# The second batch's key products moved into the first transform, in place of warm-up products; weight roundings moved beside the second layer; activation tables loaded in idle stretches

## The chip, the cores and the metric

One core of one Trainium2 chip (trn2), float32 throughout. The time is the device time of one execution, in microseconds (us), as the median of several executions. Ratios are the mean time of one kernel's fast runs over the mean time of the other's fast runs of the same rounds, with a 95% interval, so they are not quite the ratio of the medians that stand beside them. A trace belongs to one execution out of several.

## The reference

Eight batches of 576 tokens with 512 columns pass through linear attention, a two-dimensional Fourier mix, a normalisation and a two-layer perceptron:

```python
q_s = softmax(q over its 64 columns);  k_s = softmax(k over the 576 tokens)
x   = q_s @ (k_s^T @ v)                        # per batch and head; 8 heads of 64
u   = x + real(fft(fft(x, over tokens), over columns))
un  = (u - mean) / sqrt(var + 1e-6)
out = u + relu(un @ w1) @ w2                   # w1 512 x 2048, w2 2048 x 512
```

The weights arrive as 64-bit floats and are turned into float32 ("rounded") on the chip, block by block, by ScalarE, VectorE and GpSimd together.

## The kernel before

Rows of several batches form groups. Group 0 runs the two layers plainly; later groups use pre-combined weights and fewer products. While TensorE runs group g, the attention and transform of the next batch are mixed in between its products. "Batch 1" is the second batch and "batch 2" the third, counting from 0. A builder with its own estimates of durations decides the final order of each engine's instructions, so build order and run order differ. Line numbers in profiles are those of the kernel named; here is what the argument touches (cuts marked).

```python
def k_exp(self, it):                                    # one key tile: 2 heads, 128 x 576
    V.reduce_max(m[:], k, axis=AX.X, negate=True)                        # "km"
    nc.scalar.activation(k, k, ACT.Exp, bias=m[:, 0:1], accum_out=rec[:, 0:1])
    ...
def k_turn(self, it):                                   # four transposes, a copy, one more
    nc.scalar.copy(ks[:, 0:4, :], pt[:])                                 # "ks <- tr"
    ...
def k_times_v(self, it):                                # five products -> "kvr"
    ...
def block(k):                                           # one block of the transform
    ... three products into pz ...
    nc.scalar.copy(paired(z), ...)                                       # "Z <- acc"
    nc.scalar.mul(paired(zt[:, at:at + Q]), ...)                         # "ZT <- acc"
    nc.scalar.copy(paired(zt[:, at + Q:at + W]), ...)                    # "ZT <- acc"
    ...
def scales(s):                                          # in norm(g)
    nc.scalar.activation(std[:, s], mv[:, s, 1], ACT.Sqrt, bias=self.eps[:, 0:1])
    ...
def normal(i):                 # g == 0: VectorE; later groups: ScalarE, "eo <- x,mv,std"
    ...
def turn(i):                   # transposes of the normalised tile, then
    nc.scalar.copy(unT[:, u:u + 3:2, :, cols], ...)                      # "unT <- tr"
...
blk.first(fetch)               # batch 0's loads, then the weights
free = blk.hold()
one, two = front(0)            # attention; transform and mixing
for step in one + two + norm(0):
    step()
```

TensorE was kept busy in the first transform by products whose results nobody uses (`self.warm(...)`), meant to keep its granted clock up (the mean was 0.97 from 0 to 61 us). Batch 1's keys were loaded and multiplied during group 0's second layer.

## Time and profile before

| | us |
|---|---|
| median, lowest, highest of the first three runs | 1142.15, 1141.45, 1142.95 |
| span of the profiled run | 1140.2 |
| first matmul of layer one (group 0) | 61.02 |
| layer one of group 0 | 56.19 |
| layer two of group 0, with batch 1 mixed in | 83.41 |
| start of group 1 | 200.62 |
| end of the last sum on VectorE | 1133.04 |

The table is read off the TensorE timeline: the first product on `unT` with 512 columns opens layer one, the first `bc<-big` with 512 columns opens layer two, the first product on `unT` with 256 columns opens group 1. A line of a timeline has the start, the duration, the engine, line and operation, the output and inputs, the shapes and the count; in brackets stands how long the engine was idle before it and which instruction ended that. The profile lines that carry the argument stand in the prediction below.

### The profile page before, as it was taken

The numbers are of one execution on the slowest core, as the hardware profiler recorded it, in microseconds if no ns is written. First come the engines' busy times: TensorE is split into PE (matmuls) and PEld (weight loads), VectorE is DVE, ScalarE is ACT, GpSimd is POOL, SyncE is SP. The second block draws the span as 40 slices with busy tenths as digits, with TensorE's granted clock in tenths as the row PEclk, the third lists the DMA queues.
The fourth block names the chain that finished last, engine by engine and source line by source line (L and its number), as shares of the span: only waits on it lengthen the run. The fifth ranks groups of instructions, "written<-read, shape, count | busy, mean of one in ns | idle before, by whom it ended". The sixth has DMA issues, their size and how long they took to land.

```text
span 1140.2 us, 14639 instructions
## 1 busy us (share of the span) xinstructions
PE 1098.6 (96%) x5472; PEld 919.1 (81%) x5472; DVE 543.4 (48%) x1110; ACT 397.7 (35%) x956; POOL 332.5 (29%) x302
## 2 busy tenths in 40 slices
PE   5899999989999999999999999999999999999997
PEld 4644556878888988888889888888889888888886
DVE  6785756488324833384435643683344352203201
ACT  6495423274124513371226322641233142201200
POOL 2075541245012600324024402260034213302320
PEclk9999999999999999999999999999999999999999
DMA  9377784463346534554356436543453344444451
GB/s 310 120 258 243 258 279 148 149 213 140 122 150 206 202 111 143 183 195 154 124 176 213 148 113 190 195 172 107 143 191 148 114 163 148 185 139 154 150 185 55
DMA packets 92549, 193.79 MB, mean 170 GB/s; under 512 B 23088, under 2 KB 59696, under 8 KB 85312
## 3 DMA queue, kind: packets, MB, share of 16 engines
q1 hardware_dynamic: 90680, 191.82, 49.5%
q10 hardware_dynamic: 1800, 1.05, 0.3%
q8 instruction: 43, 0.70, 0.2%
q14 instruction: 26, 0.21, 0.1%
HBM read 168.72 MB, written 28.31 MB: 173 GB/s over the span
## 4 chain that ended last, share of the span: by engine, by line
PE 79%; DVE 11%; ACT 4%; DMA 2%; issue 2%; POOL 1%; SPq 0%; ACTq 0%; POOLq 0%; DVEq 0%
PE bb L850 14%; PE bb L886 13%; PE bc L886 10%; PE bc L850 9%; PE ba L850 9%; PE ba L886 8%; PE acc L484 3%; PE acc L564 2%; PE bc L789 2%; PE acc L655 2%; PE acc L658 2%; PE acc L678 1%; PE tr L750 1%; PE tr L532 1%; PE tr L467 1%
## 5 line engine op out<-in xcount | busy, mean ns | idle before, releaser
L850 PE MATMUL bb<-unT,big 128*128 128x256 f32 x768 | 187.9, 381 | 0.3 <-DVE u L822 0.3
L886 PE MATMUL bb<-big 128*128 128x256 f32 x768 | 172.8, 379 | 0.0
L850 PEld LDWEIGHTS bb<-unT,big 128*128 128x128 f32 x768 | 142.8, 190 | 23.8 <-DVE u L818 3.4
L886 PEld LDWEIGHTS bb<-big 128*128 128x128 f32 x768 | 145.1, 190 | 20.1
L341 POOL TENSOR_TENSOR big<-big 128x512 f32<-128x512 f32 (+1 forms) x38 | 45.1, 1187 | 309.5 <-ACT big L862 305.6
L850 PE MATMUL bc<-unT,big 128*128 128x256 f32 x512 | 125.3, 379 | 0.0
L850 PE MATMUL ba<-unT,big 128*128 128x256 f32 x512 | 124.3, 379 | 0.0
L862 ACT ACTIVATE big<-big 128x512 f32<-128x512 f32 x96 | 60.2, 628 | 171.3 <-DVE big L861 171.0
L886 PE MATMUL bc<-big 128*128 128x256 f32 x512 | 116.5, 379 | 0.5 <-DVE x L903 0.5
L886 PE MATMUL ba<-big 128*128 128x256 f32 x512 | 114.1, 379 | 0.0
L886 PEld LDWEIGHTS bc<-big 128*128 128x128 f32 x512 | 95.9, 190 | 14.1 <-DVE x L903 0.9
L886 PEld LDWEIGHTS ba<-big 128*128 128x128 f32 x512 | 95.9, 190 | 12.3
L850 PEld LDWEIGHTS bc<-unT,big 128*128 128x128 f32 x512 | 95.5, 190 | 12.5
L850 PEld LDWEIGHTS ba<-unT,big 128*128 128x128 f32 x512 | 95.0, 190 | 11.7
L822 DVE TENSOR_TENSOR u<-bb,s 128x512 f32<-128x512 f32 x40 | 27.6, 689 | 134.8 <-PE bb L886 79.1
L521 ACT ACTIVATE q<-q,qm 128x64 f32<-128x64 f32 x240 | 61.5, 337 | 10.2 <-DVE qm L519 9.4
L349 POOL TENSOR_TENSOR unT<-unT 128x512 f32<-128x512 f32 x8 | 14.2, 1773 | 172.9 <-DVE unT L348 172.9
L818 DVE TENSOR_TENSOR u<-bb,s 128x512 f32<-128x512 f32 x40 | 27.6, 690 | 76.8 <-PE bb L850 38.1
L898 POOL TENSOR_TENSOR x<-x,u 128x512 f32<-128x512 f32 x14 | 17.7, 1267 | 148.2 <-DVE u L822 118.0
L861 DVE TENSOR_TENSOR big<-bc,u 128x512 f32<-128x512 f32 x64 | 44.1, 688 | 26.1 <-PE bc L850 25.3
L814 ACT COPY s<-ba 128x512 f32<-128x512 f32 x40 | 23.4, 584 | 89.4 <-PE ba L886 45.5
L754 ACT COPY unT<-tr 128x512 f32<-128x512 f32 x36 | 20.6, 585 | 86.5 <-PE tr L750 86.0
(221 smaller groups left out, 1656.7 us busy)
## 6 DMA issues: line engine op xcount, KB each, us to landing
big<-w1s SPq DMA_DIRECT2D x64, 896.0 KB
big<-w2s SPq DMA_DIRECT2D x56, 1024.0 KB
big<-in_w_dram SPq DMA_DIRECT2D x21, 512.0 KB
k<-in_kT_dram SPq DMA_DIRECT2D x26, 288.0 KB
q<-in_q_dram SPq DMA_DIRECT2D x27, 256.0 KB
v<-in_v_dram SPq DMA_DIRECT2D x26, 256.0 KB
words<-in_w_dram SPq DMA_DIRECT2D x11, 512.0 KB
w2s<-big SPq DMA_DIRECT2D x8, 512.0 KB
```

The source lines that it names most:

```text
L341: e1.tensor_tensor(out=to(4), in0=at(2), in1=at(3), op=ALU.add)
L484: nc.tensor.matmul(pk, lhsT=ks[:, c, :], rhs=v[:, c, :], start=(c == 0), stop=(c == NC - 1))
L521: nc.scalar.activation(heads[:, h, :], heads[:, h, :], ACT.Exp, bias=m[:, h:h + 1])
L564: nc.tensor.matmul(px[:, r * P:(r + 1) * P], lhsT=qT[:, r, :], rhs=self.kvr[b % 2][:, r, :], start=True, stop=True)
L655: nc.tensor.matmul(full[:, at:at + size], lhsT=t[:, own], rhs=self.ft[:, f + at:f + at + size], start=at == 0, stop=False, skip_group_chec ...
L814: nc.scalar.copy(temp("s1"), box["ba"][:])
L818: V.tensor_tensor(out=temp("u2"), in0=box["bb"][:], in1=box["s1"][:], op=ALU.add)
L822: V.tensor_tensor(out=temp("u3"), in0=box["bb"][:], in1=box["s1"][:], op=ALU.add)
L850: nc.tensor.matmul(bank()[:, i, :], lhsT=w[:, WA_AT[m], k * P:(k + 1) * P], rhs=unT[:, B_AT[m], k, :], start=first and i == 0 and k == 0, ...
L861: V.tensor_tensor(out=hp(i), in0=bank[:], in1=u[:], op=ALU.add)
L862: nc.scalar.activation(hp(i), hp(i), ACT.Relu)
L886: nc.tensor.matmul(bank()[:, i, :], lhsT=h[p][:, A_AT[m], i * P:(i + 1) * P], rhs=w[:, p, :], start=first and i == 0 and p == 0, stop=p == ...
```

## The change

The intent: TensorE is idle for a third of the first 61 us and full afterwards, so work taken from the full stretch into the early one should shorten the whole. The core of the diff (cut):

```diff
+        for r in range(NR):                      # in first(): batch 1's k and v ahead of the weights
+            load(self.second_at[0][:, r * S:(r + 1) * S], self.kT[1, cols, :])
+            ...
+    def second_keys(self):                       # maxima, exponentials, square-root table load, products
+        ...
-                if b == 0:
-                    self.warm(x[:, 0:HD], 3)     # warm-up products of the mixing
-            self.wait_for(eo[1][:, NN:], [self.raws[i] for i in range(4)])
+            self.wait_for(eo[1][:, NN:], [self.raws[0]])          # 1 block rounded here, not 4
+                if i == 0:
+                    self.gate(un[:], words[0:1, 1:4, 0:2])        # blocks 1-3 wait for the first un
+            if g > 0:                            # in norm: Exp table right behind the square root
+                nc.scalar.activation(t[:], std[:, 0:1], ACT.Exp, scale=0.0)
-        held = {12: [("k", S, 2)] * 2, 14: [("q", D, 3)] * 3}
+        held = {12: [("q", D, 3)] * 3, 15: [("k", S, 2)] * 2 + [("v", NC * P, 2)] * 2}
+            order = (1, 0) if last and m == 3 else (0, 1)         # tail: the halves change places
-        return folds + [lambda k=k: block(k) for k in (2, 3, 0, 1, 4)]
+        return folds + [lambda: None] * (b > 1) + [lambda k=k: block(k) for k in (2, 3, 0, 1, 4)]
-    for step in one + two + norm(0):
+    for step in one + keys + two + products + norm(0):
-            n = 2 * NF - 8
+            n = 2 * NF - 14                      # fewer roundings beside layer one, more beside layer two
```

## The prediction

> **What bounds the kernel now.** I read the page first, then stretches of the span, then the TensorE timeline with its waits, then ScalarE, VectorE and the DMA issues around each wait, and the end of the chain of waits. From the page and from the stretches (columns: us, then busy us and count of PE, PEld, DVE, ACT, POOL, then granted clock, DMA share, GB/s):

> ```profile
> PE 1098.6 (96%) x5472; PEld 919.1 (81%) x5472; DVE 543.4 (48%) x1110; ACT 397.7 (35%) x956; POOL 332.5 (29%) x302
> ...
> 0.00:61.00 61.00, 40.52 (x234) 33.76 (x235) 44.12 (x127) 36.11 (x102) 10.28 (x30) 0.97 0.65 204
> 61.00:117.20 56.20, 55.23 (x128) 24.34 (x129) 36.03 (x65) 40.02 (x71) 35.84 (x30) 1.00 0.78 253
> 117.20:200.60 83.40, 79.22 (x329) 47.29 (x328) 55.49 (x130) 31.70 (x88) 31.94 (x38) 1.00 0.68 232
> 200.60:1128.00 927.40, 919.59 (x4768) 810.75 (x4766) 406.88 (x789) 289.91 (x696) 254.49 (x205) 1.00 0.46 159
> 1128.00:1140.20 12.20, 4.07 (x18) 2.96 (x16) 0.85 (x2) 0.00 (x0) 0.00 (x0) 0.80 0.16 43
> ```

> TensorE sets the time from 61 us on: the first layer of group 0 runs to 117.2, its second layer, with all of batch 1's attention and transform mixed in, to 200.6, the other groups to 1132.6. After 200.6 only 7.8 us are idle before 1128. Before 61 us TensorE is idle for 20.5 us, and some of the rest is junk. So two things pay: work taken out of the full stretch into the first 61 us, and waits removed. The TensorE timeline shows both:

> ```profile
> 46.52 0.61 PE L678 MATMUL acc<-cd,Z 127*128 127x127 f32 x4
> 49.48 7.13 PE L206 MATMUL tr<-x,ident 128*128 128x256 f32 x24 [2.35 <-DVE x L696]
> ...
> 61.02 3.67 PE L780 MATMUL ba<-unT,big 128*128 128x512 f32 x8 [1.11 <-ACT unT L754]
> ...
> 99.97 3.67 PE L780 MATMUL bc<-unT,big 128*128 128x512 f32 x8 [0.94 <-ACT big L782]
> ...
> 126.63 1.38 PE L484 MATMUL acc<-v,ks 128*128 128x128 f32 x10 [2.69 <-ACT ks L468]
> 127.85 0.60 PE L467 MATMUL tr<-ident,k 128*128 128x128 f32 x4
> 128.28 0.27 PE L474 MATMUL tr<-ident,k 128*128 128x128 f32 x1
> ...
> 147.60 0.49 PE L564 MATMUL acc<-kvr,qT 128*128 128x128 f32 x2 [1.48 <-DVE kvr L487]
> ```

> L206 are the warm-up products. L467, L474 and L484 are batch 1's key products inside the second layer, with a 2.69 us wait in front, because k and v of its last heads arrive only after 117 us. Between 47 and 59 us VectorE sets the pace (11.97 us busy of 12 from 46 to 58): rounding, mixing, statistics, normalising.

> Last, one table load in the loop (ScalarE, then TensorE) and the end:

> ```profile
> 229.93 1.28 ACT L457 ACT_TABLE_LOAD   x1
> ...
> 232.14 0.66 PE L467 MATMUL tr<-ident,k 128*128 128x128 f32 x4 [1.47 <-ACT k L457]
> ```

> ```profile
> 1132.62 0.42 DVE L903 TENSOR_TENSOR x<-bc,x 128x256 f32<-128x256 f32 x1 [3.81 <-PE bc L886]
> 1133.11 0.33 SPq L939 DMA_DIRECT2D mirror<-x  x1
> 1134.82 0.67 SPq L941 DMA_DIRECT2D out_dram<-mirror  x1
> ```

> [...] behind the 2.35 us gap the granted clock was 0.50 in 50:52, and 24 warm-up passes took 7.13 us where 24 x 0.215 = 5.2 would do. [...] a Relu stood behind a rounding that waited for weights, so an instruction placed early can block a later one. [...] The loads here measure 1283 each[...]. [...] this trace moves 348 to 356 from 18 to 30 us.

> **The change part by part.**

> (a) Key products of batch 1. One head pair costs 0.43 (four transposes) + 0.11 + 1.11 (ten passes at 130.11 to 131.22) = 1.65 us; four are 6.6 us out of the full stretch. The waits 2.69 and 1.48 belong to the same chain: removed. The second layer falls from 83.4 to 83.4 - 6.6 - 4.2 = 72.6 us.

> (b) Their loads, 2.5 MB, stand ahead of the weights. Only 0.66 MB of them came early before, so the opening transfer ends some 5 us later (1.8 MB at 350 GB/s), at 41 instead of 36 us. The keys land near 23 us, before they are needed at 29.4. DMA was idle from 36 to 47, so this is free.

> (c) The front. The four maxima (0.67 each, 2.7 us) fit a VectorE gap of 2.93 us before 32.33; the four exponentials and the square-root table fit a ScalarE gap of 6.43 us before 40.48. The table load at 40.86 leaves the transform's copies, and only one block is rounded there instead of four. VectorE then starts mixing about 0.75 us earlier and drops two roundings further on: un is ready about 2 us earlier. But all key products stand before the un transposes on TensorE. Each head pair is a chain: transposes 0.55, two ScalarE copies with latency about 1.05, ten passes 1.1, so 2.7 us; four of them from 47.2 end at 58. ScalarE is first blocked by half of a weight block (its order puts that conversion before the first key copy) that lands near 48.5, which adds about 1 us, and statistics and three roundings stand in the same queue before the last copies. I put the first matmul of layer one at 62.3, 1.3 later than now.

> (d) First layer: 16 x 3.43 = 54.9 us. It took 56.2, with 1.1 us of waiting on roundings. The build order has 27 blocks rounded in this stretch against 30 (the rest move beside layer two, five really, not ten, as the scheduler pulls others forward), so that wait should go. It ends at 117.2 as before: (c) and (d) cancel.

> (e) Second layer: 72.6 us, plus new waits. Work there gets shorter but the DMA does not: about 12.4 MB (combined weights out, reloads, three late blocks) must pass before the temporaries of the third combining step are free, and VectorE's order puts batch 1's folds behind that step. At 350 GB/s from 118 us that is 153.5 at the earliest (158.3 now), then about 7 us of folds; TensorE asks for them at 163.4. Also a key exponential of batch 2 now stands between two transform copies and waits for a late load. I allow 2 us (0 to 5). Group 1 then starts at 117.2 + 72.6 + 2 = 191.8 instead of 200.6: -8.8 us.

> (f) Exp table loaded right after each square root. Three waits of TensorE on the key exponential (1.47 at 232, and 1.04 + 0.19 at both 478 and 722) are 3.9 us; about 3.7 go. But the load stands before the normalising activations: their start moves by about 1.0 us. Slack there is 0.8 at 313 and 557 and none at 802.5 (a wait of 0.39 already), so 0.2 + 0.2 + 1.0 come back. Net -2.3. The one-step delay of the folds removes the waits of 0.16 at 770 and 0.55 at 889: I take -0.4.

> (g) Tail: the last product's halves change places, so the last store is one transfer instead of two. From the store's issue at 1133.11 to the second issue took 1.71 us: about -1.9 with the simpler write.

> Sum: -8.8 - 2.3 - 0.4 - 1.9 = -13.4 us, so 1128.7. I round towards caution to 1129.5, since (c) and (e) have more ways to go wrong than right.

> **The rivals.**
> R1: the ScalarE and TensorE chain of key products delays layer one by more than 1.3 us (cold clock between the sparse products, in-order conversions). For it: TensorE would be about 60% busy from 47 to 58, and 2.35 us idle already halved the clock once. Against it: a similar density from 18 to 33 us kept the clock at 1.00. It would give 1131 to 1134.
> R2: layer two becomes bound by DMA and combining, not TensorE. For it: DMA share 0.9 and more from 144 to 160, a 9.74 us VectorE wait on a weight store at 158. Against it: with fewer key operations in VectorE's queue the combining should start its stores up to 9 us earlier. At worst all the gain of (a) beyond about 4 us is lost: 1133 to 1136.
> R3: all goes through and the front even shortens by 2 us, as un is ready sooner: 1124 to 1126.
> R4: the Exp loads cost as much as they save, at every group boundary: +2 on my number.

> **Range and chances.** The gain is capped: key work and its waits 10.8, table waits 3.9, tail about 2, small ones 1, a front gain of at most 3: 21 us, or 1.8%. So faster by over 2% (under 1119.3) would need something that I don't see: 0.04. Slower by over 2% would need a stall over 23 us in a kernel whose steady part is unchanged: 0.02. All rivals lie between 1124 and 1136, which is my range.

> **What would show each step right or wrong.** (a) No key products between 117 and 200 us, and that stretch near 73 to 75 us. (b) Opening transfer ending near 41 us. (c) First layer-one matmul at 61.5 to 63.5, its wait put on the unT copy. (d) Layer one 55 us long. (e) The waits of the transform's products in layer two sum to under 3 us; a single wait over 4 us on a fold or on a Z copy is R2. (f) No TensorE wait on a key exponential, a longer one at the even group boundaries. (g) From the last VectorE sum to the end about 5.3 us instead of 7.2. I am wrong if the first group starts layer one after 65 us, or if group 1 starts after 196 or before 188 us.

## The result, and the profile after

The changed kernel took 1135.32 us (median of 4 runs, 1134.85 to 1136.85), the kernel before 1142.31 (4 runs, 1141.45 to 1142.95): ratio 0.9942, interval 0.9924 to 0.9959. It is a little faster, inside the 2% band and inside the predicted range, but 5.8 us above the point predicted. The profiled run was the slowest of the four (1136.85).

| | before | predicted | after |
|---|---|---|---|
| first matmul of layer one | 61.02 | 62.3 | 65.56 |
| layer one | 56.19 | 54.9 | 56.59 |
| layer two | 83.41 | 74.6 | 79.94 |
| start of group 1 | 200.62 | 191.8 | 202.09 |
| group 1's start to the last sum's end | 932.42 | -2.7 | 927.92 (-4.50) |
| last sum's end to the end | 7.16 | -1.9 | 5.09 (-2.07) |

The headline part gained nothing in this trace: group 1 starts 1.5 us later than before. All of the 5.1 us of shorter span come from the small parts behind it. The same stretches of the changed kernel (columns as in the prediction):

```profile
0.00:65.56 65.56, 43.19 (x271) 36.88 (x271) 44.55 (x130) 43.29 (x122) 9.71 (x32) 0.94 0.65 207
65.56:122.15 56.59, 56.59 (x128) 24.89 (x129) 34.60 (x58) 41.55 (x83) 33.07 (x28) 0.97 0.70 228
122.15:202.09 79.94, 74.82 (x270) 41.13 (x268) 51.21 (x117) 26.81 (x67) 35.54 (x41) 0.98 0.68 233
```

The granted clock (third number from the right) is below 1.00 in each of these three stretches; before, it was 1.00 in layers one and two. Layer two still has 5.1 us in which TensorE does nothing.

The TensorE timeline of the changed kernel shows the front:

```profile
47.96 0.60 PE L517 MATMUL tr<-ident,spare 128*128 128x128 f32 x4
...
50.67 1.92 PE L531 MATMUL acc<-spare,ks 128*128 128x128 f32 x10 [2.00 <-ACT ks L518]
52.38 1.06 PE L517 MATMUL tr<-ident,spare 128*128 128x128 f32 x4
...
54.12 1.67 PE L531 MATMUL acc<-spare,ks 128*128 128x128 f32 x10 [0.46 <-ACT ks L518]
...
61.05 1.04 PE L805 MATMUL tr<-ident,eo 128*128 128x128 f32 x8
63.30 1.15 PE L805 MATMUL tr<-ident,eo 128*128 128x128 f32 x8 [1.21 <-ACT unT L809]
65.56 5.08 PE L835 MATMUL ba<-unT,big 128*128 128x512 f32 x8 [1.11 <-ACT unT L809]
```

The first key product waits 2.00 us for a copy on ScalarE. The work behind it runs at half clock (0.50 from 51.33 to 54.74 us): 1.92 us for ten passes that take 1.38 further on, 1.06 us for four transposes that take 0.60. The key chain ends at 61.05 instead of the predicted 58, and the first group of layer one takes 5.08 us where the kernel before took 3.67. ScalarE in the same stretch tells why the copy was late:

```profile
48.16 0.37 ACT L732 COPY sn<-acc 128x256 f32<-128x256 f32 x1 [0.52 <-PE acc L725]
49.48 0.67 ACT L347 ACTIVATE big<-big 128x512 int32<-128x512 uint32 x1 [0.95 <-DMA big<-in_w_dram]
50.05 0.56 ACT L518 COPY ks<-tr 128x512 f32<-128x512 f32 x1
...
60.09 0.65 ACT L342 ACTIVATE bb<-big 128x512 f32<-128x512 f32 x1
...
62.66 0.59 ACT L809 COPY unT<-tr 128x512 f32<-128x512 f32 x1
```

At 49.48 half of a rounding, which has nothing to do with the keys, stood ahead of the key copy and waited 0.95 us for its own transfer; the copy could have started at 48.5. At 60.09 and after, three more pieces of rounding (L342; L347 at 60.77; the third at 61.35) stood ahead of the first unT copy.

In layer two the TensorE timeline of the changed kernel has one large wait, with slow work behind it:

```profile
180.28 0.76 PE L701 MATMUL acc<-ft,eo 128*128 128x144 f32 x4 [2.75 <-ACT ZT L712]
180.88 1.00 PE L704 MATMUL acc<-ft,eo 128*128 128x289 f32 x2
181.67 3.27 PE L844 MATMUL bc<-big 128*128 128x512 f32 x4
...
200.41 0.66 PE L805 MATMUL tr<-ident,eo 128*128 128x128 f32 x4 [0.95 <-ACT eo L799]
201.60 0.66 PE L805 MATMUL tr<-ident,eo 128*128 128x128 f32 x4 [0.53 <-ACT eo L799]
```

and ScalarE, from which it comes:

```profile
178.93 0.77 ACT L507 ACTIVATE k<-k,km 128x576 f32<-128x576 f32 x1 [4.92 <-DVE km L505]
...
179.70 0.35 ACT L707 COPY Z<-acc 127x256 f32<-127x256 f32 x1
...
195.52 1.28 ACT L785 ACT_TABLE_LOAD   x1
196.81 0.20 ACT L785 ACTIVATE root<-std 128x1 f32<-128x1 f32 x1
196.92 1.50 ACT L799 ACTIVATE eo<-x,mv,std 128x512 f32<-128x512 f32 x2
```

L507 is the exponential of a key of batch 2, which nobody needs before group 1. It stands in ScalarE's queue between two Z copies and holds the queue for 4.92 us, because its maximum comes late. VectorE reaches that maximum only at 178.15 (0.74 us), behind combining steps that wait for stores (1.17 us at 174.99). In the five other traces with this queue order (sections 1 and 3 below: headline part alone, quiet front, block 16's fetch, half of the products, junk products) that maximum itself waits 0.90 to 2.54 us for the key's own load. TensorE's next transform product waits for the ZT copy behind it all, and its clock halves (0.50 from 181.04 to 184.45 us): 3.27 us for four passes that take 1.88 elsewhere. At 195.52 the new Exp table load stands ahead of the normalising activations (L799), for which TensorE then waits 0.95 and 0.53 us; in the kernel with the headline part alone, which has no such load, it waits 0.24 and 0.54 us there.

The end, as predicted, needs one store behind the last sum instead of a copy and a store:

```profile
1129.59 0.42 DVE L960 TENSOR_TENSOR x<-bc,x 128x256 f32<-128x256 f32 x1 [3.81 <-PE bc L943]
1130.09 0.34 ACTq L992 DMA_DIRECT2D out_dram<-x  x1
1130.48 0.63 ACTq L998 DMA_DIRECT2D out_dram<-mirror  x1
```

### The profile page after: what moved, and what is told of

It reads as the page before. It is cut to its first block, busy times and chain, and to the rows that moved or that the text cites.

```text
span 1135.1 us, 14578 instructions
## 1 busy us (share of the span) xinstructions
PE 1096.6 (97%) x5448; PEld 916.9 (81%) x5448; DVE 533.4 (47%) x1094; ACT 404.6 (36%) x975; POOL 332.2 (29%) x304
## 3 DMA queue, kind: packets, MB, share of 16 engines
q10 hardware_dynamic: 1800, 1.05, 0.3%
## 4 chain that ended last, share of the span: by engine, by line
PE 83%; DVE 4%; DMA 3%; ACT 2%; issue 2%; POOL 1%; SPq 0%; POOLq 0%; ACTq 0%; DVEq 0%
PE bb L905 15%; PE bb L943 15%; PE bc L943 10%; PE ba L943 10%; PE bc L905 10%; PE ba L905 9%; PE acc L531 3%; PE acc L613 2%; PE acc L725 1%; PE acc L701 1%; PE acc L704 1%; DMA w2s<-big 1%; PE bc L844 1%; PE tr L805 1%; PE tr L581 1%
## 5 line engine op out<-in xcount | busy, mean ns | idle before, releaser
L354 POOL TENSOR_TENSOR big<-big 128x512 f32<-128x512 f32 (+1 forms) x38 | 46.4, 1220 | 281.4 <-ACT big L917 273.9
```

The source lines that it names most:

```text
L354: e1.tensor_tensor(out=to(4), in0=at(2), in1=at(3), op=ALU.add)
```

## The experiments

The theory after the result: two instructions stand at the wrong place in ScalarE's queue, roundings in the front and a key exponential in layer two, and hold up what stands behind them (waits of 0.95 us at 49.48 and of 4.92 us at 178.93); their waits also cost clock. Rivals: the clock is the first cause in the front (second half of R1); layer two is bound by its transfers and combining, so that any wait removed comes back (R2); the Exp loads cost what they save (R4). Twelve kernels ran, each beside runs of the kernel before on the same chip. All results were correct.

### 1. The parts alone

The tail alone on the kernel before:

```diff
+            order = (1, 0) if last and m == 3 else (0, 1)
         ...
+            return [lambda i=i, q=q: run(i, q) for i in order for q in range(2)]
```

> The kernel before with the swapped halves of the last product alone. Step (g) of the prediction and every theory expect the same: from the last VectorE sum to the end about 5.1 us instead of 7.2, and the time 1.9 to 2.1 us below that of the kernel before, nothing else changed. If the gain is under 1 us, the tail that I read from the two traces was not worth what it seemed.

Measured: 1141.32 us against 1143.42, ratio 0.9989 (0.9977 to 1.0001), so -1.3 us and an interval that just reaches zero. The trace shows the size better: from the last sum's end (1133.52) to the end (1138.8) 5.28 us, where the kernel before had 7.16: -1.88. The tail does what was predicted.

The Exp load alone on the kernel before:

```diff
+            if g > 0:
+                nc.scalar.activation(t[:], std[:, 0:1], ACT.Exp, scale=0.0)
```

> The kernel before with the Exp table loaded right behind each square root and nothing else. Step (f): 3.7 us of TensorE waits on key exponentials gone, 1.4 us given back by normalising activations that start later: -2.3 us. Rival R4 (the loads cost as much as they save): 0 plus or minus 0.5. In the trace step (f) has no table load ahead of a key exponential and no TensorE wait on one.

Measured: 1141.09 against 1143.42, ratio 0.999 (0.997 to 1.001). This does not tell -2.3 from 0; the single runs spread from 1138.12 to 1145.7. The spread goes with the mean granted clock that was recorded for each run: three runs at 0.996 to 0.997 took 1138.12 to 1139.65 us, where three runs of the kernel before at 0.997 took 1141.45 to 1142.16; the other three, at 0.991 to 0.994, took 1142.52 to 1145.70. That speaks for a gain near the expected one, but so few runs don't prove it. One trace shows that a saving can be given back: the builder ordered the queries anew, and a wait of 2.07 us on a query at 499 us was followed by a granted clock of 0.57 from 500 to 504.

The headline part alone, which is the changed kernel without tail, Exp load and delay of the folds:

```diff
-            order = (1, 0) if last and m == 3 else (0, 1)
+            order = (0, 1)
-            if g > 0:                 # the Exp load
+            if g > B:
-        return folds + [lambda: None] * (b > 1) + ...
+        return folds + ...
```

> The changed kernel without the swapped tail, without the Exp loads and without the one-step delay of the folds: what is left is batch 1's keys in the first transform and the moved roundings. The prediction's steps (a) to (e) give -8.8 us against the kernel before. The stages of the changed kernel's trace give about +1.5 at the start of group 1 (layer one starts 4.5 us later, layer two is only 3.5 us shorter), so between -1 and +1.5 us. If it measures -1 to +1.5, the headline part was worth nothing and the whole gain is from the small parts.

Measured: 1140.68 against 1143.42, ratio 0.9976 (0.9958 to 0.9993): -2.7 us, between 0.8 and 4.8. That is a larger gain than the -1 to +1.5 I read off one trace, and far from -8.8. In this kernel's trace group 1 starts at 199.74, layer one at 64.75, and the wait on a ZT copy is there again (2.84 us).

### 2. The key exponential in layer two

First the blunt way: batch 2's first key tiles are not even loaded before batch 1's tokens are mixed.

```diff
-        held = {12: [("q", D, 3)] * 3, 15: [("k", S, 2)] * 2 + [("v", NC * P, 2)] * 2}
+        held = {12: [("q", D, 3)] * 3, NF: [("k", S, 2)] * 2 + [("v", NC * P, 2)] * 2}
-            side = one + two + norm(1)
+            side = one + two + [lambda: free(NF)] + norm(1)      # free(NF) reads the last mixing
```

> The changed kernel with the tiles of batch 2's first keys held until batch 1's tokens are mixed, so that no key exponential of batch 2 can stand in ScalarE's queue ahead of the copies of Z. My theory (in-order ScalarE queue): the wait of 2.75 us on a Z copy at 180.28 goes, and with it the stretch at half clock behind it (1.00 and 3.27 us where 0.5 and 1.9 are usual, about 1.9 us): 3 to 4.6 us less than the changed kernel, layer two 75.5 to 77 us instead of 79.9. Rival R2 (layer two bound by the transfers and the combining): the wait reappears on a fold or on Z, layer two stays within 1 us of 79.9.

Measured: 1136.13 against 1143.42, ratio 0.9949 (0.9936 to 0.9961), no better than the changed kernel's 0.9942. The local expectation held: no wait on Z, layer two 74.53 us instead of 79.94, group 1 at 196.50. But group 2 starts at 326.32, later than the 325.85 of the changed kernel, because group 1 now takes 6.06 us longer. The wait had moved. TensorE in group 1 of this kernel:

```profile
225.05 1.11 PE L517 MATMUL tr<-ident,k 128*128 128x128 f32 x4 [2.31 <-ACT k L507]
...
226.84 2.50 PE L531 MATMUL acc<-v,ks 128*128 128x128 f32 x10 [0.46 <-ACT ks L518]
229.14 1.91 PE L905 MATMUL ba<-unT,big 128*128 128x256 f32 x4
```

The second key's maximum now runs on VectorE at 223.36 instead of 178.15, its exponential follows, TensorE waits 2.31 us for it, and the work behind is slow: 2.50 us for ten passes that take 1.38 elsewhere, 1.91 for four that take 1.03.

Then the fine way. The key is loaded and its maximum taken as early as before, but the exponential is tied to the last Z. TensorE's build order stayed the same, instruction by instruction, and ScalarE's changed in layer two by exactly this one move.

```diff
         V.reduce_max(m[:], k, axis=AX.X, negate=True)
+        if it == ("k", 2, 1):
+            self.gate(self.Zr[0:1, 0:1], m[0:1, :])   # m | (Zr & 0): the same value, ordered behind Zr
```

> The changed kernel with one thing more: the maximum of batch 2's second key waits for the last of batch 1's Z, so that its exponential stands in ScalarE's queue behind the Z copies instead of between two of them; TensorE's build order is the same instruction by instruction. Theory of the in-order queue: the TensorE wait of 2.75 us on a Z copy goes with the half-clock stretch behind it, layer two takes 75 to 77 us instead of 79.94, and as the key is still loaded early, group 1 does not lengthen (it did by 6 us where the tiles themselves were held): 3 to 4.6 us less than the changed kernel, so about 1131 us. Rival (group 1 ends when its transfers and its second batch's loads let it, whatever its start): group 2 starts at 325.8 again and nothing is gained, so about 1135.

Measured: 1132.56 (1132.36 to 1133.96) against 1142.37, ratio 0.9917 (0.9902 to 0.9931). ScalarE of this kernel has all Z copies first and waits afterwards, where nobody minds:

```profile
179.04 0.36 ACT L707 COPY Zr<-acc 1x256 f32<-1x256 f32 x1 [1.28 <-PE acc L704]
...
182.93 0.78 ACT L507 ACTIVATE k<-k,km 128x576 f32<-128x576 f32 x1 [3.37 <-DVE km L473]
```

Layer two takes 77.13 us, with no wait on a Z or ZT copy and a clock of 1.00 from 178 to 186; group 1 takes 123.77, as in the changed kernel (123.76). So 2.8 us of layer two were the position of one instruction. The ratio's interval still overlaps that of the changed kernel (0.9924 to 0.9959), and so does that of each front repair in section 3: the size of a single repair rests on the traces, and only both together (section 4) are clear of noise by the times. Rival R2 falls in its strong form: transfers and combining are untouched and the wait is gone. They have a part in it, as they made the maximum late; the queue passed the delay on to TensorE.

### 3. The front

Roundings out of the way of the key copies and the unT copies:

```diff
-                if i == 0:
+                if i == 3:                    # blocks 1-3 wait for the last un, not for the first
                     self.gate(un[:], words[0:1, 1:4, 0:2])
         ...
+            if i == 0:                        # block 16's fetch waits for it too
+                blk.gate(blk.last_un[:], blk.w2sb[0:1, 0, 0:2])
```

> The changed kernel with blocks 1 to 3 gated on the last normalised tile and block 16's fetch held behind it, so that no rounding stands in ScalarE's queue between the key copies and the unT copies. If ScalarE's queue is what delays layer one (first matmul at 65.56 instead of the predicted 62.3), the first wait of 2.00 us on a ks copy falls to about 1 us, the waits of 1.21 and 1.11 us on unT to about 1 together, and the first matmul of layer one comes at 63 to 64; layer one may wait for the late blocks, up to 1 us. If the cold clock or the chain of key products itself sets it, the first matmul stays at 64.5 to 65.6.

Measured: 1133.16 (1131.86 to 1136.86) against 1142.37, ratio 0.9923 (0.9902 to 0.9944); first matmul of layer one at 60.92. TensorE of this kernel:

```profile
46.55 0.60 PE L517 MATMUL tr<-ident,spare 128*128 128x128 f32 x4
...
47.82 1.38 PE L531 MATMUL acc<-spare,ks 128*128 128x128 f32 x10 [0.57 <-ACT ks L518]
...
50.54 1.38 PE L531 MATMUL acc<-spare,ks 128*128 128x128 f32 x10 [0.79 <-ACT ks L518]
...
60.92 3.67 PE L836 MATMUL ba<-unT,big 128*128 128x512 f32 x8 [1.10 <-ACT unT L810]
```

The key chain starts at different times in different executions (46.4 to 49.1 us in these traces). What compares is its length, from the first key transpose to the first matmul of layer one: 17.60 us in the changed kernel, 14.37 here. The chain I had put at 2.7 us per head pair is 2.72 here (47.82 to 50.54). Layer two gained nothing: it took 80.55 us, with a wait of 3.29 us on the ZT copy.

Only one of the two holds, that of block 16's fetch:

```diff
+            if i == 0:
+                blk.gate(blk.last_un[:], blk.w2sb[0:1, 0, 0:2])
```

> Only block 16's fetch is held behind the norm; the three blocks before the unT copies stay. ScalarE's order moves by one instruction: the half rounding that waited 0.95 us for its transfer ahead of the first key copy. If this head-of-line wait (and the half clock that follows the TensorE wait of 2.00 us) is the larger part of the lost front, the first wait on a ks copy falls to 0.6, the cold passes of 52 to 54 us go, and the first matmul of layer one comes at 62 to 63; the wait of 1.21 us on unT stays. If the three roundings before the unT copies are the larger part, it comes above 63.5.

Measured: first matmul at 61.95, chain 15.13 us. So of the 3.23 us, 2.47 were the one half rounding that stood ahead of the first key copy, with the half clock behind it, and 0.76 the three roundings before the unT copies. The time, 1135.84 (ratio 0.9929, 0.9912 to 0.9945), is hardly better than the changed kernel's: in this trace the wait on the ZT copy was 4.78 us, with 6.8 us of half clock behind it, and layer two took 82.89. The second bottleneck took the gain of the first. The earlier start of layer two alone does not set the size of that wait: the quiet front began layer two 2.2 us earlier still and waited 3.29.

Half of the key products moved behind the norm, between the first groups of layer one (two key tiles lie elsewhere in memory for it):

```diff
-        return [maxima, exps], pipelined(items, both)
+        return [maxima, exps], pipelined(items[:2], both), pipelined(items[2:], both)
         ...
             up[f]()
+            if f < len(others):
+                others[f]()
```

> The changed kernel with the key products of head pairs 0 and 1 alone ahead of the first norm; pairs 2 and 3 stand between the first groups of layer one, where TensorE is never idle. If the chain of four pairs (2.7 us each, predicted to end at 58, ended at 61.05) is what delays layer one, the first matmul of layer one comes at 59.5 to 61, layer one lengthens by 3.3 us (two pairs at 1.65), and layer two starts at 119 to 120.5 instead of 122.15: about -2. If VectorE's statistics set the start, it stays above 62 and the 3.3 us are lost.

Measured: 1137.67 (ratio 0.996, 0.993 to 0.999). The first matmul came at 60.62 as expected, but layer one took 60.70 us instead of the expected 59.9, 2.11 of them waits. At 121.32 layer two began only 0.8 us earlier than in the changed kernel. This way pays back what it gains.

Junk products (10 in all, 128 x 256) where TensorE waits for the key copies:

```diff
         nc.scalar.copy(ks[:, 0:4, :], pt[:])
+        if it[1] == 1:
+            for _ in range(4 if it[2] == 0 else 2):
+                nc.tensor.matmul(junk, lhsT=self.ident[:], rhs=k[:, 0:2 * P], start=True, stop=True)
```

> The changed kernel with 10 junk products between the transposes and the products of the key pairs, where TensorE waits for the copies. Cold-clock theory (rival R1's second half): the granted clock stays at 1.00 from 47 to 66 us, the first pair's products fall from 1.92 us and the second's from 1.67 to about 1.3, the first group of layer one from 5.08 to 3.67 us: -1.5 to -2.5 us at the start of layer two. If the clock costs nothing here, the start of layer two does not move or comes later by the junk's own time.

Measured: 1136.52 (ratio 0.995, 0.9932 to 0.9968), the same as the changed kernel within the interval. The clock was 1.00 throughout from 38 to 70 us, the products took 1.38 and the first group 3.67, as expected. Layer two started 1.7 us earlier, but only 0.22 us of that is the chain (17.38 instead of 17.60); 0.95 is its earlier start in this execution, and the rest is layer one, whose first group ran at full clock. That first group took 3.67 us without any junk in the repaired key kernel too, so its half clock comes and goes.

That the chain stayed as long does not clear the clock, because ScalarE's order changed too. In the changed kernel the products of the four head pairs start at 50.67, 54.12, 57.12 and 59.84, so the two pairs at half clock cost 3.45 and 3.00 us instead of 2.72: 1.0 us. With the junk they start at 49.72, 52.43, 55.15 and 58.69: that 1.0 us is gone, and 0.8 us came back in the last pair, whose copy now stands behind two pieces of a rounding (56.10 and 56.69):

```profile
56.10 0.66 ACT L342 ACTIVATE bb<-big 128x512 f32<-128x512 f32 x1 [0.40 <-DVE big L473]
```

```profile
58.69 1.38 PE L536 MATMUL acc<-big,ks 128*128 128x128 f32 x10 [0.75 <-ACT ks L518]
```

So both halves of R1 hold. Of the 2.47 us that the misplaced half rounding cost, 1.4 were the longer wait (2.00 instead of 0.57) and 1.0 the half clock behind it.

### 4. Both repairs together

The edits of the fine key repair and of the quiet front, and two variants of the Exp load on top: behind the last normalising activation, or none at all.

```diff
+ the edits of the fine key repair (2) and of the quiet front (3)
  # variant "behind the norm":
-            if g > 0:
-                nc.scalar.activation(t[:], std[:, 0:1], ACT.Exp, scale=0.0)
+            if g > 0 and i == 3:                  # after the last normal(i)
+                nc.scalar.activation(t[:], un[:, 0:1], ACT.Exp, scale=0.0)
  # variant "no Exp load":
-            if g > 0:
+            if g > B:
```

> The changed kernel with the two repairs that worked alone: no roundings before the unT copies in ScalarE's queue, and the key exponential of batch 2 behind the Z copies. If they are the two separate causes that I hold them for (one in the front, one in layer two), they add up: first matmul of layer one at 61, layer two from 116.5, about 77 us long, group 1 at 193.5 to 194.5, and the time 7 to 8 us below the changed kernel, 1127 to 1128.5. If the second stage takes back what the first gains (layer two bound by the transfers and the combining, rival R2), layer two lengthens to 80 us or more and the time is 1130 to 1132.

> The same with the Exp table loaded behind the last normalising activation instead of ahead of the first. In the changed kernel's trace the load of 1.28 us at 195.52 stands before them, and TensorE waits 0.95 and 0.53 us on normalised tiles: these 1.5 us should go at the start of group 1, and up to 1 us at each later even boundary where there is no slack: 1 to 3 us below the kernel with both repairs. If the load's place costs nothing (slack everywhere), no difference.

> The kernel with both repairs without the Exp loads of the change: step (f) of the prediction puts them at -2.3 us (3.7 saved, 1.4 given back), so this one should be 2 to 2.5 us slower than the kernel with both repairs. Rival R4 (they cost as much as they save): equal within 0.5 us.

| | median (lowest to highest) | ratio to the kernel before | layer two | start of group 1 |
|---|---|---|---|---|
| both repairs | 1128.75 (1128.45 to 1129.10) | 0.9868 (0.9853 to 0.9883) | 75.12 | 194.06 |
| and Exp load behind the norm | 1129.0 (1128.09 to 1131.59) | 0.9874 (0.9858 to 0.9890) | 74.55 | 190.86 |
| and no Exp load | 1130.25 (1129.75 to 1131.74) | 0.9883 (0.9869 to 0.9898) | 74.41 | 192.80 |

The kernel before ran at 1143.46. Both repairs give -15 us, 1.3%; the changed kernel had 0.6%. The start of group 1 came as expected (194.06; expected 193.5 to 194.5); layer two began 2.4 us later than expected and was 1.9 us shorter (75.12 instead of about 77); the time is 0.25 us above the range expected. This is the fastest kernel. The profiled run of "both repairs" had by chance a half clock from 18 to 26 us, so its key chain started at 49.08; the chain was 14.37 us and layer one 55.49. Its stretches:

```profile
63.45:118.94 55.49, 55.28 (x129) 24.25 (x130) 35.26 (x59) 43.32 (x86) 35.11 (x29) 1.00 0.71 232
118.94:194.06 75.12, 72.87 (x269) 40.55 (x268) 51.27 (x118) 27.02 (x67) 35.31 (x41) 1.00 0.72 249
```

Layer two no longer takes anything back: 75.12 us although it began 3.2 us earlier than in the changed kernel, and the clock is 1.00 in both. By the ratios the two repairs together gain more (0.0074) than the sum of each alone (0.0025 and 0.0019). In the traces the quiet front alone made layer two 0.6 us longer, the key repair alone 2.8 shorter, and both 4.8 shorter, which fits; but the intervals, each about 0.002 wide to either side, don't prove it.

Without the Exp loads the kernel was 1.7 us slower by the ratios (0.0015 of 1143.46). The intervals overlap, so R4 is not excluded by the times. The traces speak for the loads: from group 1's start to TensorE's end 927.57 us with them and 931.17 without, -3.6, against +0.7 in layer two, where the load delays the normalising activations. That is -2.9 net, where step (f) had -2.3. Loading behind the norm gave no gain: the builder ordered the queries differently, a wait of 2.03 us on a query appeared at 488, and group 1 took 124.97 us instead of 123.76.

## Why the prediction was right or wrong

The time fell in the range and "within 2%" was right, but two of the signs I had set for being wrong came true: layer one started after 65 us, and group 1 after 196. Against the unrounded sum of 1128.7 the profiled run (1136.85) is 8.2 us late. The steps account for it: +4.95 at the start of layer two (122.15 instead of 117.2), +5.34 in layer two, -1.8 in the loop, -0.2 in the tail, together +8.3. That the time stayed inside the range is partly luck: the range allowed for R1 or R2, both came together, and the profiled execution (1136.85) lies outside it. The headline part, which was to bring 8.8 of the 13.4 us, brought 2.7 when it ran alone (0.8 to 4.8).

- (a) The mechanism was right: no key product is left between 117 and 200 us, and with the waits repaired layer two takes 74.4 to 75.1 us, where I had 74.6 with 2 us of waits; without its waits it is 72.87 us of busy TensorE (both repairs), where I had 72.6.
- (b) Right: the transfers ran at 299 GB/s from 36 to 41 us and at 13 from 41 to 43. The prediction's 350 GB/s was an estimate from the kernel before, which moved 351 GB/s from 18 to 30 us; the same trace has 407 GB/s from 126 to 128 us. Batch 1's keys and values are 2.36 MB (eight tiles of 128 x 576 in float32), not 2.5, which changes the 5 us by 0.4.
- (c) Mis-sized: +1.3 us predicted, +4.54 measured. The step said that half a weight block would block ScalarE first and add "about 1 us". It measured 2.47 (chain 17.60 against 15.13 without it): 1.4 for TensorE's wait of 2.00 instead of 0.57, and 1.0 for the slow products behind it, which the term left out. My 47.2 to 62.3 is a chain of 15.1, so about 14.1 without that block; it measured 15.13, and 14.37 once the three roundings before the unT copies were gone too. The chain also started 0.76 us late (47.96 instead of 47.2): this execution ran at half clock from 38 to 41 us, and of the eight traces that did not, seven started it at 46.4 to 47.1 (the eighth, both repairs, had its half clock earlier).
- (d) The wait on roundings did go, as predicted. But layer one took 56.59 instead of 54.9, since its first group ran at half clock (5.08 instead of 3.67). With the repairs it took 55.49.
- (e) This is the term that cost most. The step named the very instruction ("a key exponential of batch 2 now stands between two transform copies and waits for a late load") and then allowed 2 us for everything. It measured 0.90 + 2.75 + 0.95 + 0.53 = 5.1 us of waits and 1.8 us of half clock behind the longest (1.00, 3.27 and 0.76 us for work that takes 0.65, 1.88 and 0.66). About 0.7 of the waits belongs to the Exp load of step (f) (0.95 and 0.53 with it, 0.24 and 0.54 without), which I had charged to later boundaries and not to this one.
- (f) Mechanism right, size too small in this trace: -4.5 us from group 1 to the last sum, where (f) had -2.3 and -0.4. My sign "no TensorE wait on a key exponential" failed in one place, 1.05 us at 232.34, where no table is loaded and the maximum itself came late.
- (g) Right: -2.07 in the trace of the changed kernel and -1.88 with the tail alone, predicted -1.9.
- R1 was right in both halves: in the changed kernel's trace ScalarE's order costs 1.4 us of wait and 0.76 before the unT copies, the half clock 1.0 us in the key chain and 1.4 in the first group of layer one. R2 was right about the loss and wrong about its owner: one move in ScalarE's queue removed the wait with all transfers left in place. R3 did not come: with both orders repaired the time is 1128.75, above its 1124 to 1126, and layer one starts at 60.8 to 63.5 us instead of 2 us earlier than the 61.02 before. R4 is unlikely but not excluded.

Why do executions with the same waits differ in their clock? The traces answer most of it. The clock records of all 14 traces show that each stretch at half clock, until the work ends, lasts 3.41 us or twice that, and that within one trace these stretches start whole multiples of 3.41 us apart (in the changed kernel at 37.68, 51.33, 64.98 and 181.04 us: 4, 4 and 34 of them), while their place against the kernel's start differs from execution to execution. On this grid of windows there are 24 drops from full to half clock between 14 and 1115 us. In the window before each of them TensorE was busy for at most 52%; only two windows under 50% (45 and 47%, both in the trace with half of the products moved) were not followed by one. Some windows and the clock behind them:

| trace and window (us) | TensorE busy, us | clock in the next 3.41 us |
|---|---|---|
| changed kernel, 34.26 to 37.68 | 1.71 | 0.50 |
| changed kernel, 47.92 to 51.33, with the wait of 2.00 | 1.41 | 0.50 |
| changed kernel, 177.62 to 181.04, with the wait of 2.75 | 0.76 | 0.50 |
| kernel before, 46.50 to 49.92, with the wait of 2.35 | 1.06 | 0.50 |
| kernel before, 121.60 to 125.01 and 125.01 to 128.42, with the wait of 2.69 across both | 2.33 and 1.79 | 1.00 and 1.00 |
| tail alone, 123.75 to 127.16, with the same wait (2.99) almost wholly inside | 0.80 | 0.50 |
| half of the products, 45.39 to 48.81 and 48.81 to 52.22, with a wait of 2.01 across both | 1.85 and 2.18 | 1.00 and 1.00 |

In these rows a wait inside one window was followed by half clock, and one spread over two was not. This is read off the traces; no run tested it by moving a wait. The length of one wait alone does not tell: 2.01 and 2.69 us passed at full clock, 2.00 and 2.75 did not. And the same waits of about 1.2 and 0.51 us in front of 38 us led to 0.50 in 3 of the 11 traces with the new front, and to 1.00 in the other 8.

That an instruction placed early on ScalarE can hold up a later one shows in two traces. In the kernel before, a rounding waited 2.00 us for its words and started at 98.12; the Relu behind it started at 99.25, and TensorE's product waited for that Relu until 99.97 (0.94 us). In the changed kernel a rounding that waited 0.95 us held the key copy behind it until 50.05. The Exp table load costs ScalarE 1.28 us in all at the start of group 1: the activation before it ends at 195.51, the load runs from 195.52 to 196.80, and the next activation starts at 196.81.

What stays open: whether the repairs are truly worth more together than apart; and what the delay of the folds and the moved weight roundings are worth, which never ran alone.
